# A fused attention and MLP kernel: seven products in the eighth step of the second layer too, and a flag that is read before the last output is evicted

## The chip, the core and the metric

The kernel runs on one core of one Trainium2 chip. A core has five engines that run side by side and meet at semaphores: TensorE (PE, with its weight loads shown as PEld), VectorE (DVE), ScalarE (ACT), GpSimd (POOL) and SyncE (SP), which here issues nearly all DMAs. TensorE reads SBUF and adds up in PSUM, which has eight banks; SBUF is the working memory, 128 partitions wide.

The metric is the device time of the whole kernel in microseconds. A profiled execution gives the trace; the times are of runs without the profiler.

## The reference

Attention with global and local keys and a distance bias, for 4 batches, 8 heads, 768 positions and 64 dimensions; then a two-layer MLP (3072 tokens, 512 to 2048 to 512) with h * tanh(softplus(h)):

```python
scores = scale * np.matmul(q, k.transpose(0, 1, 3, 2)) + bias     # bias: -slope * distance
scores = np.where(keep, scores, -1000000000.0)                    # keep: 8 global keys, 96 local ones
a = np.exp(scores - np.max(scores, axis=-1, keepdims=True))
x = np.matmul(a / (np.sum(a, axis=-1, keepdims=True) + 1e-09), v) # then (tokens, 512)
h = x @ w_in
g = h * np.tanh(np.where(h > 20.0, h, np.log1p(np.exp(np.minimum(h, 20.0)))))
return (g @ w_out).astype(np.float32)
```

## The kernel before

**Precision.** A float32 operand is split into a high and a low float16 part, and a product is three matmuls: high x high, high x low, low x high.

**Tiling.** The tokens run in 12 chunks (`ci`, 0 to 11) of 256, two blocks of 128 each. A chunk is attention first: scores, maximum, exponent, the split of the weights into halves (`hl`), their transposition by a DMA (`AT`), the product with v, the division (`x`), and the split and transposition of x (`xhl`, `xT`). Then the MLP runs in eight steps (`fp`, 0 to 7) of 256 hidden columns; step number m = 8 ci + fp. A step is a first-layer product on TensorE (`ph`, 24 matmuls of 256 columns), four ScalarE passes and one VectorE pass for the activation (`gf`), the split into halves (`gt`), and the second-layer product, which adds into the chunk's PSUM banks over its eight steps.

**Seven products.** A second-layer step is a 2 x 2 block product: two blocks of 128 tokens, two blocks of 128 hidden columns, and two halves (`HN` = 256) of the 512 outputs. Written out it is 8 block products, done as 12 matmuls of 512 columns (L726). From chunk 3 on, steps 0 to 6 form it from 7 block products instead, 21 matmuls of 256 columns (L717), after a scheme that needs sums of blocks: `sums_g` (L617 to L619) makes them from the activations for every step, and `whole_w`, `sums_w`, `high_s`, `low_s` once from the weights of that step. `FAST` says from which chunk each step does so; for step 7 it is `NC`, so never. The products go to four banks: 0 and 1 hold the two token blocks' own parts, 2 and 3 parts that both share. Steps 0 to 6 fill banks 2 and 3; step 7 writes banks 0 and 1 alone. So `corner` can take banks 2 and 3 to SBUF (`corners`, four pieces of 256 columns; L739 to L741) while step 7 still runs, and `evacuate` adds them to banks 0 and 1 on the way out (L753).

**The flag.** This path is valid for certain arguments and values only. Sums of everything that could have gone wrong are tested (`checks`), a scalar `done_i` is made from the tests, and behind the schedule all engines load it (L73) and branch (L74): to the end, or to a slow general kernel, `dense`. Steps k0, k1 and k3 make and test the indicators of all but the last chunk's output; k2 stands last, behind the last eviction: a matmul over the sums that the last evictions made (L807), two VectorE operations (L809, L810).

**Order.** `PROGRAM` is the order, written out by hand as some 2,100 tokens: a letter for an action, a number for chunk, block or step, and an apostrophe for the other of two engines that can do it. Each engine takes its instructions in the order in which the tokens issue them. The letters that matter here: i first-layer product, j, u, n, r, H activation, J sums of blocks, z and Z high and low halves, o second-layer product, I corner, Q eviction, Y store, g, p, X attention weights' split and transposition, T, U, V the same for x, P, G, e, m the sums and halves of the weights, w, q, v loads, O a product that only keeps TensorE busy, k checks.

Of the kernel before, what the change touches and what calls it, by code (L numbers as in the profile page):

```python
# [42 lines left out]
def tile_kernel(ctx, tc, qd, kd, qT, kT, v, n, w_in, w_out, out):  # L43
# [29 lines left out]
    left = nc.values_load(done_i[0:1, 0:1], min_val=0, max_val=1)  # L73
# [35 lines left out]
def windowed(st, tc, loc):  # L109
# [36 lines left out]
    nc.vector.memset(busy, 0.0)
# [389 lines left out]
    def high_x(n, other=False):  # L536
# [165 lines left out]
    PRODUCTS = ((0, 0, 2, 0), (2, 2, 0, 0), (6, 3, 0, 1), (1, 5, 1, 0), (3, 1, 3, 1), (5, 6, 2, 1), (4, 4, 3, 0))  # L702

    def moe_out(m):
# [8 lines left out]
        if fast(m):  # L713
            for i, k, bank, side in PRODUCTS:
                w = factor(fp, k)
                for n, (x, y) in enumerate(((0, 0), (0, 1), (1, 0))):
                    nc.tensor.matmul(pos[ci][bank][:, side * HN:(side + 1) * HN], gt[:, x, i, :], w[y], start=not begun[ci][bank], stop=n == 2 and fp == NFP - 2 and (i, k) in ((5, 6), (4, 4)))  # L717
                    begun[ci][bank] = True
            return
        for bank in range(2):  # L720
            for j in range(2):
                fb = 2 * fp + j
                for n, (x, y) in enumerate(((0, 0), (0, 1), (1, 0))):
                    cols = (slice(0, HN), slice(HN, DM)) if bank == 1 and begun[ci][1] and j == n == 0 and len(pos[ci]) > 2 else (slice(0, DM),)
                    for c in cols:
                        nc.tensor.matmul(pos[ci][bank][:, c], gt[:, x, 2 * j + 1 - bank, :], wv4[:, 2 * fb + 1, y, c], start=not begun[ci][bank], stop=last and j == 1 and n == 2)  # L726
# [6 lines left out]
    def corner(ci, other=False):  # L733
# [6 lines left out]
        nc.vector.scalar_tensor_tensor(c[:, 1:3, :], end, BACK, c[:, 3:4, :].broadcast_to([P, 2, HN]), op0=ALU.mult, op1=ALU.add)  # L740
        nc.vector.scalar_tensor_tensor(c[:, 3, :], end[:, 1, :], BACK, c[:, 1, :], op0=ALU.mult, op1=ALU.add)  # L741

    def evacuate(ci):
        po = pos.pop(ci)
        obs[ci] = raws.tile([P, DM, 2], I32, name="wr", bufs=3).bitcast(F32).rearrange("p f w -> p (f w)").rearrange("p (t m) -> p t m", t=2)
        for bank in range(2):
# [4 lines left out]
            else:  # L751
                c = corners[ci]
                nc.vector.scalar_tensor_tensor(obs[ci][:, t].rearrange("p (b m) -> p b m", b=2), po[bank].rearrange("p (b m) -> p b m", b=2), BACK, c[:, bank:bank + 3:2, :], op0=ALU.mult, op1=ALU.add, accum_out=osum[:, n:n + 1])  # L753
# [285 lines left out]
```

## Time and profile before

| what | value |
|---|---|
| median of 3 runs | 595.21 us (594.56 to 596.01) |
| the profiled execution, in all | 594.36 us |
| its span, first to last instruction | 592.5 us |
| DMA moved in the span | 73.76 MB, mean 124 GB/s |
| granted TensorE clock, mean | 1.0 |
| largest group, first-layer matmuls (L583) | 265.6 us |

The table goes from whole to part. The span is what the trace covers; the profiled execution's own time has 1.9 us more around it. TensorE's clock stands at full speed in all of the profile's slices.

### The profile page before, as it was taken

To read this page: it belongs to the slowest core of one execution; us is meant where nothing else is said; L and a number is where in the kernel's file an instruction comes from. 1 tells how busy PE (TensorE), PEld (TensorE's weight loads), DVE (VectorE), ACT (ScalarE), POOL (GpSimd) and SP (SyncE) were. 2 spreads that over 40 slices of the span, in tenths; PEclk is the share of its full clock that TensorE was granted. 3 is DMA by queue.
4 is the path that set the end of the run, shared out by engine and by line. 5 is a ranking of instruction groups with operands and counts; after the bars stand their busy time and mean duration, and the time that the engine had idled before them with its cause. 6 is when DMAs were issued, how large, how long until landed. Compare 5 with 4: busy or idle time off the path is not lost.

```text
span 592.5 us, 14936 instructions
## 1 busy us (share of the span) xinstructions
PE 577.9 (98%) x5652; PEld 466.6 (79%) x5652; DVE 489.3 (83%) x1272; ACT 478.3 (81%) x1112; POOL 261.3 (44%) x259
## 2 busy tenths in 40 slices
PE   6999999999999999999999999999999999999996
PEld 4887866567667789788889788888888888888884
DVE  6999999998999999989888986687888876663665
ACT  6999999999898998896786697677888678765661
POOL 0145422236316876552443474555563433444251
PEclk9999999999999999999999999999999999999999
DMA  9999999562562448654753653554574414240001
GB/s 228 312 276 191 254 308 242 151 148 66 118 150 55 114 95 137 100 117 122 166 115 68 126 127 80 94 118 107 88 178 58 101 38 90 54 91 19 36 2 38
DMA packets 132972, 73.76 MB, mean 124 GB/s; under 512 B 102144, under 2 KB 122624, under 8 KB 132896
## 3 DMA queue, kind: packets, MB, share of 16 engines
q1 hardware_dynamic: 132608, 72.63, 54.6%
q8 instruction: 45, 0.74, 0.5%
q14 instruction: 31, 0.25, 0.1%
q10 hardware_dynamic: 288, 0.14, 0.1%
HBM read 38.62 MB, written 6.29 MB: 76 GB/s over the span
## 4 chain that ended last, share of the span: by engine, by line
PE 77%; DVE 7%; DMA 6%; ACT 4%; issue 2%; POOL 2%; SPq 1%; DVEq 0%; POOLq 0%; ACTq 0%
PE ph L583 35%; PE pav L717 13%; PE po L717 10%; PE po L726 6%; PE sc L434 4%; PE sc L522 3%; PE pav L726 3%; DMA AT<-hl 2%; DMA vc<-v 2%; DMA wts<-w_in 1%; PE pav L518 1%; DMA qr<-qT 1%; DVE gf L607 1%; DVE gt L157 1%; DVE hl L157 1%
## 5 line engine op out<-in xcount | busy, mean ns | idle before, releaser
L583 PE MATMUL ph<-xT,wts 128*128 128x256 f16 x2304 | 265.6, 273 | 2.7 <-DVE gf L607 2.5
L583 PEld LDWEIGHTS <-wts 128*128 128x128 f16 x2304 | 222.3, 98 | 35.4 <-issue 5.4
L717 PEld LDWEIGHTS <-gt 128*128 128x128 f16 x1323 | 127.7, 98 | 16.7 <-issue 2.0
L157 POOL TENSOR_TENSOR gt<-gf,gt 128x896 f16<-128x896 f32 (+1 forms) x40 | 72.0, 1803 | 71.5 <-DVE gt L151 48.3
L590 ACT ACTIVATE e<-ph 128x512 f32<-128x512 f32 x96 | 56.4, 588 | 58.3 <-PE ph L583 55.9
L457 ACT ACTIVATE A<-A,nm 128x232 f32<-128x232 f32 (+1 forms) x192 | 88.3, 462 | 17.5 <-DVE nm L448 17.3
L607 DVE SCALAR_TENSOR_TENSOR gf<-e,ph 128x512 f32<-128x512 f32 x96 | 65.5, 682 | 32.1 <-ACT e L602 19.1
L157 POOL TENSOR_TENSOR hl<-A,hl 128x512 f16<-128x512 f32 (+1 forms) x39 | 47.5, 1224 | 78.5 <-DVE hl L151 48.4
L448 DVE CUSTOM_DVE_ANT_0 A<-sc,mb 128x232 f32<-128x232 f32 (+1 forms) x192 | 63.4, 375 | 11.7 <-PE sc L434 6.7
L726 PEld LDWEIGHTS <-gt 128*128 128x128 f16 x405 | 38.5, 98 | 40.8 <-issue 0.4
L598 ACT ACTIVATE e<-e,part 128x512 f32<-128x512 f32 x96 | 68.8, 717 | 2.1
L594 ACT ACTIVATE e<-e,ones 128x512 f32<-128x512 f32 x96 | 68.8, 717 | 1.8
L726 PE MATMUL po<-wts,gt 128*128 128x512 f16 (+1 forms) x309 | 68.4, 373 | 0.0
L157 DVE TENSOR_TENSOR gt<-gf,gt 128x896 f16<-128x896 f32 (+1 forms) x56 | 60.3, 1079 | 8.2 <-ACT gt L153 7.6
L157 POOL TENSOR_TENSOR wts<-ws,wts 128x512 f16<-128x512 f32 x22 | 30.0, 1366 | 74.0 <-ACT wts L153 28.0
L717 PE MATMUL pav<-wts,gt 128*128 128x256 f16 x378 | 62.0, 273 | 0.0
L602 ACT ACTIVATE e<-e 128x512 f32<-128x512 f32 x96 | 59.9, 624 | 1.7
L717 PE MATMUL po<-wts,gt 128*128 128x256 f16 x378 | 51.6, 273 | 0.0
L617 POOL TENSOR_TENSOR gf<-gf 128x128 f32<-128x128 f32 x41 | 23.2, 566 | 54.1 <-DVE gf L607 52.3
L151 DVE TENSOR_SCALAR gt<-gf 128x896 f16<-128x896 f32 (+1 forms) x51 | 31.5, 619 | 15.3 <-POOL gf L619 8.8
L153 ACT ACTIVATE gt<-gf 128x896 f16<-128x896 f32 (+1 forms) x45 | 36.5, 812 | 7.2 <-POOL gf L619 3.4
L457 ACT ACTIVATION_READ_ACCUMULATOR A<-A,nm 128x1 f32 x192 | 36.2, 189 | 0.0
(173 smaller groups left out, 900.8 us busy)
## 6 DMA issues: line engine op xcount, KB each, us to landing
qr<-qT SPq DMA_DIRECT2D x24, 256.0 KB
wts<-w_in SPq DMA_DIRECT2D x12, 512.0 KB
wts<-w_out SPq DMA_DIRECT2D x12, 512.0 KB
kr<-kd SPq DMA_DIRECT2D x32, 184.0 KB
out<-wr SPq DMA_DIRECT2D x11, 512.0 KB
vr<-v SPq DMA_DIRECT2D x10, 512.0 KB
vc<-vo SPq DMA_DIRECT2D x15, 192.0 KB
wr<-w_in SPq DMA_DIRECT2D x4, 512.0 KB
```

The source lines that it names most:

```text
L153: nc.scalar.activation(out, in_, AF.Copy, scale=scale)
L157: (nc.vector if other else nc.gpsimd).tensor_tensor(out, in_, high, op=ALU.subtract)
L448: nc.vector.tensor_tensor_reduce(out=A[:, j, 0:w], in0=sc[j][:, 0:w], in1=m, scale=-1.0 / (UNIT if ci < CF32 else UNIT * SQ), scalar=3.0e3 ...
L457: nc.scalar.activation(A[:, j], A[:, j], AF.Exp, bias=nm[:, h:h + 1], scale=-1.0, accum_out=rs[:, h:h + 1])
L583: nc.tensor.matmul(ph[:, j, :].rearrange("p (b t) -> p b t", b=2), wv4[:, 2 * fb, x, c * P:(c + 1) * P], xT[:, :, y * NCC + c, :], start=( ...
L590: nc.scalar.activation(mish[m]["e"], mish[m]["h"], AF.Exp, scale=1.0 / (SV * SW), accum_out=esum[:, m:m + 1])
L594: nc.scalar.activation(e, e, AF.Square, bias=ones)
L598: nc.scalar.activation(e, e, AF.Ln, bias=part, scale=SV * SW / SG / 2.0)
L602: nc.scalar.activation(e, e, AF.Exp, scale=-1.0)
L607: nc.vector.scalar_tensor_tensor(gf, mish[m]["e"], SG / (SV * SW), mish[m]["h"], op0=ALU.subtract, op1=ALU.mult, accum_out=gsum[:, m:m + 1])
L717: nc.tensor.matmul(pos[ci][bank][:, side * HN:(side + 1) * HN], gt[:, x, i, :], w[y], start=not begun[ci][bank], stop=n == 2 and fp == NFP ...
L726: nc.tensor.matmul(pos[ci][bank][:, c], gt[:, x, 2 * j + 1 - bank, :], wv4[:, 2 * fb + 1, y, c], start=not begun[ci][bank], stop=last and ...
```

## The change

Five things change.

1. `FAST` is 3 for all eight steps: step 7 of chunks 3 to 10 makes 7 products as well. The very last step (m = 95) is left out by `fast`; its products for the second token block are cut into column halves, the first half complete before the second is begun. A chunk whose eight steps are all of seven products is a `whole_chunk` (3 to 10).
2. The products within a step stand in another order: bank 2 first, then 3, 0 and 1. In a whole chunk banks 2 and 3 close in step 7 and not in step 6.
3. In a whole chunk, `corner` writes one quarter of the output itself, with its sum into `osum3`, and `evacuate` the other three quarters. `corner` now stands behind the chunk's last product.
4. The last chunk's evictions have no sum. The flag tests instead the activations: `gsum` times 0 plus `esum`, summed (`worst`, in k1), so all is known before step 95's products. The load of the flag is token k4, ahead of Q11; its bounds test is left out.
5. Split copies of x take their buffers from the ring of three of the attention weights (`hl`) and no longer from two of their own; a buffer `four` holds step 7's weight sums. `PROGRAM` is written anew throughout.

```diff
-    left = nc.values_load(done_i[0:1, 0:1], min_val=0, max_val=1)
+        left = windowed(st, tc, locals())
...
-    FAST = (3,) * 7 + (NC,)
+    FAST = (3,) * 8
...
+    four = cp.tile([P, 2, 4, DM // 2], F16, name="four")
...
-        xhl = at.tile([P, 2, DM], F16, name="xhl")
+        xhl = at.tile([P, 2, 2, W], F16, name="hl", bufs=3).rearrange("p a b w -> p a (b w)")
...
-        return ci >= FAST[fp]
+        return ci >= FAST[fp] and m != NC * NFP - 1
+
+    def whole_chunk(ci):
+        return all(fast(ci * NFP + fp) for fp in range(NFP))
...
-    PRODUCTS = ((0, 0, 2, 0), (2, 2, 0, 0), (6, 3, 0, 1), (1, 5, 1, 0), (3, 1, 3, 1), (5, 6, 2, 1), (4, 4, 3, 0))
+    PRODUCTS = ((0, 0, 2, 0), (5, 6, 2, 1), (3, 1, 3, 1), (4, 4, 3, 0), (2, 2, 0, 0), (6, 3, 0, 1), (1, 5, 1, 0))
...
-            for i, k, bank, side in PRODUCTS:
+            ends = {2: 1, 3: 3} if fp == NFP - 2 and not whole_chunk(ci) else {2: 1, 3: 3, 0: 5, 1: 6} if last else {}
+            for q, (i, k, bank, side) in enumerate(PRODUCTS):
...
+        end = ci == NC - 1 and last
+        for bank, c in ((0, slice(0, DM)), (1, slice(0, HN)), (1, slice(HN, DM))) if end else ((0, slice(0, DM)), (1, slice(0, DM))):
...
+        if whole_chunk(ci):
+            into, total = out_tile(ci)[:, 0, HN:], osum3[:, ci:ci + 1]
+            nc.vector.scalar_tensor_tensor(into, end[:, 1, :], BACK, c[:, 1, :], op0=ALU.mult, op1=ALU.add, accum_out=total)
+            return
...
+                pieces = (slice(0, 1),) if bank and whole_chunk(ci) else (slice(0, 1), slice(1, 2)) if bank and ci == NC - 1 else (slice(0, 2),)
+                for k in pieces:
+                    total = osum[:, n:n + 1] if ci < NC - 1 else None
...
-            nc.vector.reduce_max(worst, esum, axis=AX.X)
+            nc.vector.scalar_tensor_tensor(seen, gsum, 0.0, esum, op0=ALU.mult, op1=ALU.add, accum_out=worst)
...
-            pe = ps.tile([1, 2], F32, name="sc")
-            nc.tensor.matmul(pe, ones, osum[:, 2 * NC - 2:], start=True, stop=True)
...
+            done.append(nc.values_load(L.done_i[0:1, 0:1], min_val=0, max_val=1, skip_runtime_bounds_check_because="the value is a product of comparisons"))
...
-        "F": lambda i: tc.mark_branch_hint_location("general", engines=[E.PE, E.Activation, E.DVE]),
+        "F": lambda i: tc.mark_branch_hint_location("general", engines=[E.PE, E.Activation, E.DVE, E.SP]),
...
-        J91 r93 H93 j92 u92 z91' n92 i94 J93' r92 j94 u94 Z91' H92 J92' o90 z92' Z92 n94 z93' r94 H94 i95 J94 o91 j95 Z93' o92 o93 z94' u95 n95 Z94 r95 H95 k1
-        z95 Z95' k3 o94 I11 o95 Q11 k2
+        F0 j93 u93 n93 Y10 J89' z89' Z90 Z89 H91 i92 r93 J91 j92 H93 z91' u92 i94 J93 n92 Z91 j94 r92 H92 o89 J92' z92' u94 o90 z93' n94 Z92' r94 o91 i95 j95
+        o92 H94 u95 J94' Z93' n95 z94' k0 Z94 o93 r95 H95 k1 z95' Z95 k3 o94 I11' o95 k4 Q11
```

What the order does at three places, in the instructions of one engine (line, operation, out<-in, size; behind an underscore is the buffer's number).

VectorE at the end of the program, before: the flag's first part, the corner of chunk 11, the two evictions with their sums (`osum`), the two operations on the check of these sums, the flag's load and the branch.

```order
L804 SCALAR_TENSOR_TENSOR v_125<-v_125,fl 1x1
L739 TENSOR_TENSOR vr<-vr 128x256
L740 SCALAR_TENSOR_TENSOR vr<-pav_8820,vr 128x512
L741 SCALAR_TENSOR_TENSOR vr<-pav_8820,vr 128x256
L753 SCALAR_TENSOR_TENSOR wr,osum<-po_8817,vr 128x512
L753 SCALAR_TENSOR_TENSOR wr,osum<-po_8818,vr 128x512
L809 TENSOR_SCALAR last<-sc 1x2
L810 SCALAR_TENSOR_TENSOR done_i<-last,v_125 1x1
L73 TENSOR_LOAD done_i
L74 COMPARE_AND_BRANCH
```

The same place after (the line numbers are the changed file's):

```order
L830 SCALAR_TENSOR_TENSOR done_i<-v_129,fl 1x1
L751 SCALAR_TENSOR_TENSOR vr<-pav_8919,vr 128x512
L756 SCALAR_TENSOR_TENSOR vr<-pav_8919,vr 128x256
L832 TENSOR_LOAD done_i
L776 SCALAR_TENSOR_TENSOR wr<-po_8916,vr 128x512
L776 SCALAR_TENSOR_TENSOR wr<-po_8917,vr 128x256 x2
L73 COMPARE_AND_BRANCH
```

The flag is complete ahead of the corner, its load has moved ahead of the evictions, these have no sum and the second is in two halves; the corner's first sum has gone to GpSimd.

VectorE at the end of chunk 10 (step 87 is its last), before: the activation of step 90, a low half, the corner on banks 2 and 3 (`pav`), the evictions of banks 0 and 1 (`po`), a check.

```order
L607 SCALAR_TENSOR_TENSOR gf,gsum<-e,ph 128x512
L157 TENSOR_TENSOR gt<-gf,gt 128x896
L740 SCALAR_TENSOR_TENSOR vr<-pav_8307,vr 128x512
L741 SCALAR_TENSOR_TENSOR vr<-pav_8307,vr 128x256
L753 SCALAR_TENSOR_TENSOR wr,osum<-po_8304,vr 128x512
L753 SCALAR_TENSOR_TENSOR wr,osum<-po_8305,vr 128x512
L784 TENSOR_SCALAR ind<-osum 128x22
```

After:

```order
L609 SCALAR_TENSOR_TENSOR gf,gsum<-e,ph 128x512
L750 TENSOR_TENSOR vr<-vr 128x256
L751 SCALAR_TENSOR_TENSOR vr<-pav_8368,vr 128x512
L754 SCALAR_TENSOR_TENSOR wr,osum_117<-pav_8368,vr 128x256
L776 SCALAR_TENSOR_TENSOR wr,osum<-po_8365,vr 128x512
L776 SCALAR_TENSOR_TENSOR wr,osum<-po_8366,vr 128x256
L151 TENSOR_SCALAR gt<-gf 128x896
```

The corner's first sum is here on VectorE, its last operation writes output, and the second eviction is half as wide. On TensorE one first-layer step (i93) stands between o87 and o88, the next chunk's first product.

SyncE at the start, before: the first loads of queries, keys, weights and values.

```order
L175 DMA qr<-qT 128x2x256
L178 DMA kr<-kd 64x2x264
L335 DMA wts<-w_in 128x4x256
L175 DMA qr<-qT 128x2x256
L178 DMA kr<-kd 64x2x264 x2
L215 DMA vo<-v 128x2x512
```

After:

```order
L1058 BRANCH_PREFETCH_HINT
L175 DMA qr<-qT 128x2x256
L178 DMA kr<-kd 64x2x264
L335 DMA wts<-w_in 128x4x256 x2
L175 DMA qr<-qT 128x2x256
L178 DMA kr<-kd 64x2x264 x2
L215 DMA vo<-v 128x2x512
```

A hint stands ahead of the first load, and a second weight load ahead of the second queries and keys and of the first values.

More of the change, by code (lines that the diff above doesn't have):

```diff
@@ L693, in factor @@
         a, b = 4 * fp + 1, 4 * fp + 3
+        if fp == NFP - 1 and k in (1, 4, 5, 6):
+            return [four[:, y, max(k - 3, 0), :] for y in range(2)]
         if k < 4:
@@ L713, in moe_out @@
         if fast(m):
-            for i, k, bank, side in PRODUCTS:
+            ends = {2: 1, 3: 3} if fp == NFP - 2 and not whole_chunk(ci) else {2: 1, 3: 3, 0: 5, 1: 6} if last else {}
+            for q, (i, k, bank, side) in enumerate(PRODUCTS):
                 w = factor(fp, k)
                 for n, (x, y) in enumerate(((0, 0), (0, 1), (1, 0))):
-                    nc.tensor.matmul(pos[ci][bank][:, side * HN:(side + 1) * HN], gt[:, x, i, :], w[y], start=not begun[ci][bank], stop=n == 2 and fp == NFP - 2 and (i, k) in ((5, 6), (4, 4)))
+                    nc.tensor.matmul(pos[ci][bank][:, side * HN:(side + 1) * HN], gt[:, x, i, :], w[y], start=not begun[ci][bank], stop=n == 2 and ends.get(bank) == q)
                     begun[ci][bank] = True
             return
-        for bank in range(2):
+        end = ci == NC - 1 and last
+        for bank, c in ((0, slice(0, DM)), (1, slice(0, HN)), (1, slice(HN, DM))) if end else ((0, slice(0, DM)), (1, slice(0, DM))):
             for j in range(2):
@@ L723, in moe_out @@
                 for n, (x, y) in enumerate(((0, 0), (0, 1), (1, 0))):
-                    cols = (slice(0, HN), slice(HN, DM)) if bank == 1 and begun[ci][1] and j == n == 0 and len(pos[ci]) > 2 else (slice(0, DM),)
-                    for c in cols:
-                        nc.tensor.matmul(pos[ci][bank][:, c], gt[:, x, 2 * j + 1 - bank, :], wv4[:, 2 * fb + 1, y, c], start=not begun[ci][bank], stop=last and j == 1 and n == 2)
+                    nc.tensor.matmul(pos[ci][bank][:, c], gt[:, x, 2 * j + 1 - bank, :], wv4[:, 2 * fb + 1, y, c], start=not begun[ci][bank], stop=last and j == 1 and n == 2 and c.stop == DM)
                     begun[ci][bank] = True
@@ L752, in evacuate @@
                 c = corners[ci]
[L753 removed]
+                pieces = (slice(0, 1),) if bank and whole_chunk(ci) else (slice(0, 1), slice(1, 2)) if bank and ci == NC - 1 else (slice(0, 2),)
+                for k in pieces:
+                    total = osum[:, n:n + 1] if ci < NC - 1 else None
+                    nc.vector.scalar_tensor_tensor(obs[ci][:, t].rearrange("p (b m) -> p b m", b=2)[:, k], po[bank].rearrange("p (b m) -> p b m", b=2)[:, k], BACK, c[:, bank:bank + 3:2, :][:, k], op0=ALU.mult, op1=ALU.add, accum_out=total)
             if ci == NC - 1:
@@ L777, in windowed @@
     worst = cp.tile([P, 1], F32, name="worst")
+    seen = cp.tile([P, NG], F32, name="seen")
+    done = []
     v1 = cp.tile([1, NX - 2], F32, name="v1")
     v2 = cp.tile([1, NC], F32, name="v2")
-    v3 = cp.tile([1, 4], F32, name="v3")
+    v3 = cp.tile([1, 3], F32, name="v3")
     def checks(i):
@@ L893, in windowed @@
                 acts[c[0]](int(c[1:]))
+    return done[0]
 def dense(st, tc, loc):
```

133 lines of the change are left out of this document (70 added, 63 removed).

## The prediction, made before the changed kernel ran

> **What bounds the kernel now.** First the page: how busy each engine is, and the chain that ended last.
>
> ```profile
> PE 577.9 (98%) x5652; PEld 466.6 (79%) x5652; DVE 489.3 (83%) x1272; ACT 478.3 (81%) x1112; POOL 261.3 (44%) x259
> PE 77%; DVE 7%; DMA 6%; ACT 4%; issue 2%; POOL 2%; SPq 1%; DVEq 0%; POOLq 0%; ACTq 0%
> ```
>
> TensorE (PE) is busy 577.9 of 592.5 us and holds 77% of the chain. Matmul ends are modelled, so I don't trust 98% alone; the list of what PE waited for decides.
>
> ```profile
> PE sc L434 <- DMA kr<-kd: 4.0, 1, 4.0
> PE ph L583 <- DVE gf L607: 2.5, 3, 1.2
> PE po L401 <- DVE AT L146: 1.3, 1, 1.3
> PE sc L807 <- DVE wr L753: 0.8, 1, 0.8
> PE sc L522 <- DMA AT<-hl: 0.8, 2, 0.4
> PE pav L518 <- DMA vc<-v: 0.7, 1, 0.7
> ```
>
> The columns are the total, the number and the longest wait. 4.0 + 1.3 us pass before the first keys are there, 0.8 us lie in the tail, and only 2.5 + 0.8 + 0.7 = 4.0 us are lost in the 580 us between. So PE's own work sets the time; a microsecond less of it is a microsecond less of span, if the new order feeds PE as well.
>
> **Term 1, the products.** A step of 8 x 3 products was merged into 12 matmuls of 512 columns, one of them cut in two; it becomes 7 x 3 = 21 matmuls of 256. Both kinds stand in the trace, the wide ones in the eighth step, the narrow ones in the seven others. Chain in order of time (start, us, what), then the timeline of PE:
>
> ```profile
> 554.29 0.98 PE pav L717 x9
> 555.27 2.59 PE po L726 x13
> ```
> ```profile
> 427.93 0.49 PE L717 MATMUL pav<-wts,gt 128*128 128x256 f16 x3
> ...
> 430.23 2.78 PE L583 MATMUL ph<-xT,wts 128*128 128x256 f16 x24
> ```
>
> The wide step takes 2.59 us. A whole narrow step runs from 427.93 to 430.23: 2.30 us, 109 ns a matmul (0.98 / 9 in the chain too). Each converted step saves 0.29 us. Chunks 3 to 10 convert, eight steps; the last step of chunk 11 stays wide (its second half is cut into halves, the same columns). 8 x 0.29 = **-2.3 us**. The upper bound of the gain is this, since no product goes elsewhere; the lower one is zero if PE waits where the work was.
>
> [...]
>
> **Term 2, the tail.** Before, the flag sums the last chunk's output: evict, matmul (L807), two VectorE operations, load of the flag, branch. Timeline, the lines L73 and L74 by themselves, and the stretches of the DMA:
>
> ```profile
> 584.68 2.76 PE L726 MATMUL po<-wts,gt 128*128 128x512 f16 x13
> 586.44 0.42 DVE L741 SCALAR_TENSOR_TENSOR vr<-pav,vr 128x256 f32<-128x256 f32 x1
> 587.47 0.69 DVE L753 SCALAR_TENSOR_TENSOR wr<-po,vr 128x512 f32<-128x512 f32 x1
> 587.49 1.05 SPq L758 DMA_DIRECT2D out<-wr  x2
> 588.63 0.21 DVE L810 SCALAR_TENSOR_TENSOR done_i<-last,v 1x1 int32<-1x1 f32 x1
> ```
> ```profile
> L73 DVEq TENSOR_LOAD <-done_i x1: 832/832/832, 588.9 to 588.9; - x1
> L74 SPq COMPARE_BRANCH  x1: 58/58/58, 590.0 to 590.0; - x1
> L74 SPq EVENT_SEMAPHORE  x8: 17/17/17, 590.5 to 591.1; - x8
> ```
> ```profile
> 589.00:590.00 1.00, 0.00 (x0) 0.00 (x0) 0.00 (x0) 0.00 (x0) 0.00 (x0) 1.00 0.75 277
> 590.00:591.00 1.00, 0.00 (x0) 0.00 (x0) 0.00 (x0) 0.00 (x0) 0.00 (x0) 1.00 0.03 8
> ```
>
> The last product ends at 584.68 + 2.76 = 587.44, the span at 592.5: 5.06 us. From SyncE's branch (590.0) to the end are 2.5 us. The second store is issued when the last eviction is done (587.47 + 0.69 = 588.16), its issue ends at 587.49 + 1.05 = 588.54, and its data move until almost 590.0: 1.8 us from the issue's start.
>
> After, call the end of the last product T. The last eviction has 256 columns: 0.42 us (L741's form), without a sum to read; the store is issued at T + 0.46 and its data landed at T + 2.3. The flag was loaded earlier, so SyncE branches behind the issue (0.38 us), at T + 0.85; by the branch alone the span would end at T + 0.85 + 2.5 = T + 3.35. But SyncE closes with eight semaphore waits (590.5 to 591.1), the stores' among them, and these now wait for the landing. What lay behind them before is 592.5 - 590.5 = 2.0 us from the first and 1.4 from the last, so the end is at T + 3.7 to T + 4.3; I take the middle, T + 4.1 with a little for completion. The tail gains 5.06 - 4.1 = **-0.95**; bounds -1.7 (branch alone) and -0.7.
>
> Two waits are added ahead of T. The check matmul (L794, L820 after) needs chunk 11's last activations. Timeline:
>
> ```profile
> 575.06 0.49 PE L717 MATMUL pav<-wts,gt 128*128 128x256 f16 x3
> 578.15 0.69 DVE L607 SCALAR_TENSOR_TENSOR gf<-e,ph 128x512 f32<-128x512 f32 x1
> 579.12 1.09 DVE L791 TENSOR_SCALAR ind<-gsum 128x94 f32<-128x94 f32 x1
> 582.03 0.41 PE L794 MATMUL sc<-ind,ones 128*1 128x145 f32 x2
> ```
>
> The last first-layer step ended at 575.06; the indicators were ready at 579.12 + 1.09 = 580.21, which is 5.15 us later, and three product steps (6.97 us) covered that. In the new program the step before, o91, stands ahead of i95, and two steps, 4.6 us, are left as cover. PE waits 5.15 - 4.6 = 0.55 us, or nothing if the 1.09 us (for 94 columns) does not recur; I take +0.3. Behind it the VectorE queue is: ten flag operations, the corner (its sum now on GpSimd, behind the last step's low half), the flag load of 0.83 us, three evictions. If the load holds the queue, bank 0's eviction starts 0.5 us late and the end with it; if it runs while the corner executes, it costs nothing. I take +0.2. Sum of the tail: -0.95 + 0.3 + 0.2 = **-0.45**, bounds -1.7 and +0.4.
>
> **Term 3, the start.** SyncE has one hint more ahead of its first load, no row of its own; between nothing and the nearest row, the branch's 58 ns, I take +0.06. It now sends a second 512 KB weight load ahead of the second pair of query and key loads and of the first values.
>
> ```profile
> 2.93 5.47 DMA qr<-qT
> 12.06 0.71 PE L434 MATMUL sc<-kr,qr 64*128 64x128 f32 x8
> 6.00:12.00 6.00, 6.00 (x25) 3.38 (x25) 5.62 (x34) 5.03 (x21) 0.00 (x0) 1.00 1.09 296
> ```
>
> At 296 GB/s, 524 KB are 1.8 us. The queries landed at 8.4, their first product ran at 12.06: 3.7 us of cover. The values have less, perhaps +0.6; against it, the 0.7 us wait for vc may go, as one weight load fewer stands ahead of it. I take 0 with these ends, and **+0.1** with the hint.
>
> **Term 4, added work on other engines.** Eight steps more need the three sums (two of 128 columns, one of 256: 0.29 + 0.43 + 0.29 = 1.0 us by the medians on VectorE), and their high and low halves have 896 columns and not 512.
>
> ```profile
> L619 DVE TENSOR_TENSOR gf<-gf x22: 291/293/1865, 188.4 to 575.4; 128x128 f32<-128x128 f32 x22
> L618 DVE TENSOR_TENSOR gf<-gf x22: 424/425/1299, 187.5 to 575.0; 128x256 f32<-128x256 f32 x22
> L641 DVE TENSOR_TENSOR vr<-wts x6: 1219/1225/1475, 138.7 to 193.9; 128x1024 f32<-128x1024 f16 x6
> 190.00:200.00 10.00, 9.28 (x116) 7.00 (x115) 9.72 (x14) 9.93 (x20) 7.99 (x8) 1.00 0.43 97
> 500.00:510.00 10.00, 10.00 (x103) 9.01 (x101) 4.93 (x16) 8.27 (x23) 3.80 (x4) 1.00 0.37 69
> ```
>
> Past 250 us VectorE has room, and a step has at least one 2.6 us first-layer step of cover, so I cost this at nothing there. The weights of the eighth step are prepared once: 1.2 us on VectorE for the whole (L641) and about as much for the low halves, near 185 us, where VectorE is 97% busy in the row of 190; that is the third rival. At a chunk's end the corner now starts behind the last products, not a step earlier:
>
> ```profile
> L153 ACT ACTIVATE vr<-pav x9: 574/580/597, 242.4 to 584.5; 128x512 f32<-128x512 f32 x9
> L740 DVE SCALAR_TENSOR_TENSOR vr<-pav,vr x9: 691/692/693, 245.1 to 585.7; 128x512 f32<-128x512 f32 x9
> L753 DVE SCALAR_TENSOR_TENSOR wr<-po,vr x18: 678/684/691, 248.3 to 587.5; 128x512 f32<-128x512 f32 x18
> ```
>
> The copy (0.58) hides beside the other banks' products, since bank 2 closes first. From bank 3's last product: sum 0.43, 0.69, 0.42, evictions 0.68 and 0.42, together 2.6 us, with three accumulators to read about 2.9; 9 products (0.98 us) still run then, so VectorE is done 1.9 us past the step. The tightest boundary, chunk 10's, has one 2.62 us step on PE there, and the next chunk writes bank 2 first. No wait, with 0.7 us to spare.
>
> **Sum:** -2.3 - 0.45 + 0.1 = -2.7 us (rounded). The profiled execution took 594.36 us in all (span 592.5); 594.36 - 2.7 = 591.7. The median of the runs shown is 0.85 above it, so on that scale 595.21 - 2.7 = **592.5**.
>
> **Rivals.**
> - *The new order also removes waits.* Of the 4.0 us of inner waits half go and the tail's two waits don't come: 592.5 - 2.0 - 0.5 = 590.0 to 591. For it: the order is new throughout. Against: nothing in the rows shows that it aims at these. 13 in 100.
> - *The preparation at 185 us is not hidden.* Its 2.5 us on VectorE all reach PE: 595.0. For it: PE already waits at 197 and VectorE is at 97%. An operation of VectorE there can take far longer than its median: L619's third number is 1865 ns against 293. [...] 19 in 100, time 594 to 596.4.
> - *Slower: the shared ring.* The 20 split copies of x lose their own two buffers and join the ring of three that the 80 attention copies turn in. Each must wait until a transposition three places back has left.
>
> ```profile
> ACT hl L153 <- DMA AT<-hl: 3.6, 3, 2.0
> DVE hl L151 <- DMA AT<-hl: 3.0, 2, 2.4
> ```
>
>   Such waits exist: 6.6 us in 5, 1.3 each, now off PE's path. If every chunk from 2 to 11 gets one and half of it reaches the chunk's first step on PE, that is 10 x 0.65 = +6.5: 599.0. It decides once it costs over 4.0 us, 0.4 a chunk. Against: PE waited only 0.8 us for these transpositions. 10 in 100.
> - *The saved products are none:* if weight loads (one for each matmul) set PE's pace, 21 loads replace 13, and the kernel is slower by 8 x 8 x 0.098 = 6.3 us less the tail: some 601. PE's spacing of 109 and 216 ns for 256 and 512 columns speaks against it. 2 in 100.
>
> ```profile
> L717 PEld LDWEIGHTS <-gt 128*128 128x128 f16 x1323 | 127.7, 98 | 16.7 <-issue 2.0 <-ACT A L457 0.2
> ```
>
> **Chances.** Forecast 56 in 100 (591 to 594.0), then 13, 19, 10 and 2. The smallest difference that a measurement here tells from none is about 0.2%, 1.2 us: 594.0 and 596.4. Faster: 54 + 13 + 3 = 70; within: 2 + 14 = 16; slower: 2 + 10 + 2 = 14. The range 590.0 to 596.0 leaves out the shared ring and the loads (12), the third rival's end (3) and some of the first's (5).
>
> **What will show it.** Right: PE's busy time lower by about 2.3 us; 21 matmuls of 256 columns at 109 ns in the eighth step from chunk 3; no matmul on osum; the flag load ahead of the last evictions; some 4.1 us from the last product to the end. Wrong: a wait of PE at the check matmul over 0.6 us; new waits of PE near 185 to 210 us, or of the first-layer matmuls (ph) at the start of chunks; waits for AT<-hl above 0.8 us on PE; waits of po or pav products for VectorE at a chunk's start.

## The result, and the profile after

| | median | runs |
|---|---|---|
| before, measured beside it | 595.19 us | 6, 594.53 to 596.36 |
| after | 599.28 us | 6, 599.02 to 600.25 |

The ratio is 1.0069, with a 95% interval from 1.0055 to 1.0082: the changed kernel is 4.1 us slower (3.3 to 4.9). The forecast was 592.5 us, from 590 to 596: the sign is wrong.

The engines' line of the page of after, whose span is 597.2 us:

```profile
PE 577.4 (97%) x5716; PEld 474.0 (79%) x5719; DVE 503.9 (84%) x1291; ACT 482.1 (81%) x1119; POOL 273.6 (46%) x271
```

Read it as span less busy time. Before, TensorE (PE) was idle for 592.5 - 577.9 = 14.6 us; now for 597.2 - 577.4 = 19.8. So 5.2 us of new idle time stand against 0.5 us less of work. VectorE (DVE) is busy 14.6 us longer, GpSimd (POOL) 12.3. What TensorE waited for, after (total, number, longest):

```profile
PE sc L436 <- DMA kr<-kd: 4.5, 1, 4.5
PE ph L585 <- DVE gf L609: 3.9, 5, 2.1
PE po L403 <- DVE AT L146: 1.3, 1, 1.3
PE ph L564 <- DVE xT L553: 1.3, 1, 1.3
PE sc L436 <- DVE xmax L535: 1.1, 1, 1.1
PE sc L436 <- DVE nm L450: 1.1, 2, 0.8
PE pav L729 <- POOL gt L157: 0.8, 1, 0.8
```

The first line is the start, where the first keys come later (4.0 before). Of the others all but the one of `po` are new or longer than before, and behind each stands VectorE or GpSimd. The busy time by stretches says where: after each stretch its length, then TensorE, its weight loads, VectorE, ScalarE and GpSimd, the granted clock and the DMA's share; before first, then after.

```profile
30.00:60.00 30.00, 29.02 (x246) 23.60 (x246) 28.83 (x89) 29.07 (x80) 15.15 (x12) 1.00 1.01 232
60.00:250.00 190.00, 187.89 (x1756) 137.23 (x1754) 180.08 (x418) 178.30 (x404) 91.77 (x80) 1.00 0.65 149
300.00:350.00 50.00, 49.98 (x534) 42.47 (x532) 42.69 (x108) 37.56 (x86) 22.79 (x24) 1.00 0.50 104
450.00:500.00 50.00, 50.00 (x538) 42.85 (x537) 37.59 (x102) 37.92 (x85) 20.61 (x23) 1.00 0.34 66
```
```profile
30.00:60.00 30.00, 27.83 (x222) 22.52 (x223) 27.80 (x83) 26.83 (x73) 12.87 (x11) 0.94 0.89 221
60.00:250.00 190.00, 187.97 (x1763) 138.49 (x1762) 178.79 (x417) 181.07 (x407) 95.95 (x84) 1.00 0.65 151
300.00:350.00 50.00, 46.70 (x514) 40.22 (x512) 44.10 (x102) 38.49 (x91) 23.32 (x27) 1.00 0.54 120
450.00:500.00 50.00, 48.87 (x537) 42.72 (x534) 42.16 (x107) 38.95 (x88) 23.92 (x22) 1.00 0.36 69
```

TensorE loses 1.2 us at 30 to 60, nothing from there to 250, 3.3 at 300 to 350, 1.1 at 450 to 500. The first stretch also shows a clock of 0.94, which the table of before never does. The timeline of TensorE there (start, duration, and in brackets the idle time ahead), and two of its stretches:

```profile
46.13 2.78 PE L585 MATMUL ph<-xT,wts 128*128 128x256 f16 x24
50.19 0.63 PE L564 MATMUL ph<-ident,x 128*128 128x128 f32 x4 [1.27 <-DVE xT L553]
51.66 2.12 PE L436 MATMUL sc<-kr,qr 64*128 64x232 f32 x8 [0.85 <-DVE nm L450]
```
```profile
52.00:54.00 2.00, 2.00 (x9) 1.21 (x8) 1.97 (x4) 2.00 (x8) 1.16 (x1) 0.53 0.83 262
54.00:56.00 2.00, 2.00 (x12) 1.45 (x11) 2.00 (x4) 2.00 (x5) 0.00 (x0) 0.61 0.21 78
```

Two waits, 1.27 and 0.85 us, and then the granted clock is one half for 3.4 us (52.1 to 55.6, read from slices of 0.5 us): eight score matmuls take 2.12 us and not 1.05. So the stop costs its 2.1 us of waits and, estimated as half of the 3.4 us, 1.7 more. Before, the product of step 0 (12 matmuls, 2.75 us) stood in this gap; now it stands at 57.8 us.

At 302 us, VectorE's queue after, then GpSimd's:

```profile
301.82 2.19 DVE L157 TENSOR_TENSOR gt<-gf,gt 128x896 f16<-128x896 f32 x1
303.94 2.07 DVE L157 TENSOR_TENSOR hl<-A,hl 128x512 f16<-128x512 f32 x1
305.93 0.67 DVE L609 SCALAR_TENSOR_TENSOR gf<-e,ph 128x512 f32<-128x512 f32 x1
```
```profile
301.18 1.89 POOL L157 TENSOR_TENSOR gt<-gf,gt 128x896 f16<-128x896 f32 x1 [1.10 <-DVE gt L151]
303.09 2.36 POOL L157 TENSOR_TENSOR wc<-kr,wc 128x736 f16<-128x736 f32 x1
```

Both low halves on VectorE lie beside one on GpSimd and take 2.19 and 2.07 us; their medians are 1.08 and 0.69. The activation (`gf`) stands behind them, and TensorE waits 2.07 us for it. The trace shows the overlap and the longer times; that the one causes the other is inferred.

Behind 250 us TensorE has four waits over 0.3 us, which end at 306.7, 342.8, 346.6 and 478.0 us. The corners of chunks 4, 5 and 8 run at 294, 343 and 476 us, so all four lie at a corner or within 13 us behind one.

### The profile page after: what moved, and what is told of

Same layout as the page of the kernel before. It is cut to its first block, busy times and chain, and to the rows that moved or that the text cites. A ratio compares the mean times of both kernels' runs of the same rounds, so it can differ in the third digit from the quotient of the medians.

```text
span 597.2 us, 15161 instructions
## 1 busy us (share of the span) xinstructions
PE 577.4 (97%) x5716; PEld 474.0 (79%) x5719; DVE 503.9 (84%) x1291; ACT 482.1 (81%) x1119; POOL 273.6 (46%) x271
## 4 chain that ended last, share of the span: by engine, by line
PE 40%; DVE 5%; ACT 2%; issue 1%; DMA 1%; POOL 1%; DVEq 0%; POOLq 0%; SPq 0%; ACTq 0%
PE ph L585 19%; PE pav L729 10%; PE po L729 7%; PE sc L436 2%; PE sc L524 1%; DMA AT<-hl 1%; DVE gt L157 1%; DVE gf L609 1%; DVE hl L556 1%; DVE gf L623 1%; ACT A L459 0%; DVE hl L157 0%; PE po L737 0%; DVE gt L151 0%; POOL gf L623 0%
## 5 line engine op out<-in xcount | busy, mean ns | idle before, releaser
L729 PEld LDWEIGHTS <-gt 128*128 128x128 f16 x1491 | 143.2, 98 | 21.5 <-issue 2.6
L157 POOL TENSOR_TENSOR gt<-gf,gt 128x896 f16<-128x896 f32 (+1 forms) x42 | 75.8, 1807 | 64.0 <-DVE gt L151 39.5
L459 ACT ACTIVATE A<-A,nm 128x232 f32<-128x232 f32 (+1 forms) x192 | 88.3, 462 | 10.7 <-DVE nm L450 10.7
L729 PE MATMUL pav<-wts,gt 128*128 128x256 f16 x402 | 66.3, 273 | 1.3 <-POOL gt L157 0.8
L157 POOL TENSOR_TENSOR hl<-A,hl 128x512 f16<-128x512 f32 (+1 forms) x31 | 36.6, 1183 | 54.5 <-DVE hl L151 30.5
L157 POOL TENSOR_TENSOR wts<-ws,wts 128x512 f16<-128x512 f32 x21 | 27.2, 1299 | 68.9 <-ACT wts L153 21.5
L622 POOL TENSOR_TENSOR gf<-gf 128x128 f32<-128x128 f32 x43 | 27.6, 641 | 67.9 <-DVE gf L609 66.8
L729 PE MATMUL po<-wts,gt 128*128 128x256 f16 x426 | 58.1, 273 | 0.0
L737 PEld LDWEIGHTS <-gt 128*128 128x128 f16 x306 | 29.3, 98 | 31.2 <-issue 0.6
L151 DVE TENSOR_SCALAR gt<-gf 128x896 f16<-128x896 f32 (+1 forms) x50 | 34.3, 688 | 16.4 <-POOL gf L624 13.1
L157 DVE TENSOR_TENSOR hl<-A,hl 128x512 f16<-128x512 f32 (+1 forms) x49 | 43.8, 898 | 4.5 <-ACT hl L153 4.2
L737 PE MATMUL po<-wts,gt 128*128 128x512 f16 (+1 forms) x210 | 46.7, 373 | 0.0
```

Source lines behind the costliest of these rows:

```text
L157: (nc.vector if other else nc.gpsimd).tensor_tensor(out, in_, high, op=ALU.subtract)
L459: nc.scalar.activation(A[:, j], A[:, j], AF.Exp, bias=nm[:, h:h + 1], scale=-1.0, accum_out=rs[:, h:h + 1])
```

## The experiments

Two theories at the start. A: the loss is in the rewritten order. B: it is in the work that the seven products add on VectorE, GpSimd and ScalarE. Third, C: the shared ring. All 18 in one table; each ratio is to the runs of before on the same chip, and the last column is the ratio less one times 595.2.

| run | what | median | ratio (95%) | us |
|---|---|---|---|---|
| after | | 599.28 | 1.0069 (1.0055 to 1.0082) | +4.1 |
| e1 | after, no seven products in the eighth steps, none of their added work | 597.24 | 1.0032 (1.0017 to 1.0047) | +1.9 |
| e13 | e1, no shared ring | 597.63 | 1.0039 (1.0025 to 1.0053) | +2.3 |
| e7 | after, added work, ordinary products | 599.12 | 1.0065 (1.0052 to 1.0078) | +3.9 |
| e3 | old order, new tail, with the hint | 595.70 | 1.0003 (0.9989 to 1.0017) | +0.2 |
| e14 | e3 + added work | 601.80 | 1.0113 (1.0094 to 1.0131) | +6.7 |
| e15 | e3 + late corners | 604.10 | 1.0152 (1.0136 to 1.0167) | +9.0 |
| e9 | e5 + ring | 617.07 | 1.0374 (1.0353 to 1.0396) | +22.3 |
| e2 | whole change in the old order | 641.59 | 1.0772 (1.0743 to 1.0801) | +46 |
| e16 | after, step 0 in the gap | 597.85 | 1.0055 (1.0038 to 1.0072) | +3.3 |
| e8 | after, six entries moved | 599.11 | 1.0065 (1.0052 to 1.0078) | +3.9 |
| e18 | e16 + e8 | 598.13 | 1.0051 (1.0039 to 1.0063) | +3.0 |
| e6 | after, front of before | 600.49 | 1.0075 (1.0057 to 1.0092) | +4.5 |
| e4 | after, third weight load put back | 606.41 | 1.0179 (1.0152 to 1.0206) | +10.7 |
| e17 | before + hint for SP | 595.64 | 1.0012 (1.0004 to 1.0021) | +0.7 |
| e5 | e3 without the hint | 594.76 | 0.9989 (0.9976 to 1.0002) | -0.7 |
| e12 | after without the hint | 600.64 | 1.0098 (1.0072 to 1.0124) | +5.8 |
| e10 | e16 without the hint | 600.84 | 1.0112 (1.0089 to 1.0136) | +6.7 |
| e11 | e1, front of e10, no hint | 597.90 | 1.0055 (1.0035 to 1.0075) | +3.3 |

### The new order or the added work (e1, e7)

e1 (the entries that go out stand here in one line):
```diff
-    FAST = (3,) * 8
+    FAST = (3,) * 7 + (NC,)
...
-  P7' G7' e7 m7' J31' J39' J47' J55' J63 J71' J79' J87
```


> The changed kernel in its new order, but the eighth step multiplies in the ordinary way (twelve products 512 wide) and the sums, the wide halves and the four prepared weight blocks that only the seven products need are left out. The output is the same. Theory A (the loss is in the rewritten order): TensorE gets 8 x 0.29 = 2.3 us more work and every wait stays, 599.3 + 2.3 = 601.6 us, and at least 600.5. Theory B (the loss is in the work that the seven products add on VectorE, GpSimd and ScalarE): the waits behind 250 us go with it, and about 596.5 us is left (595.2 plus 1.3 for the late start). In the profile, A still has the waits of TensorE near 302 and 476 us, B has not.

e7, with the entries kept, the halves of the eighth steps still seven blocks wide:
```diff
-        return slice(1, 8) if fast(m) else slice(0, 4)
+        return slice(1, 8) if fast(m) else slice(0, 7) if padded(m) else slice(0, 4)
```


> The changed kernel in its new order, and with the added work of VectorE, GpSimd and ScalarE (sums, halves seven blocks wide, four prepared blocks, whose results aren't used), but the eighth step multiplies in the ordinary way. Theory B1 (the added work makes the waits behind 200 us): the waits at 302, 343, 346 and 476 us stay and TensorE gets 2.3 us more, 599.3 + 2.3 = 601.6 us. Theory B2 (the shorter products uncover work that was there anyway): the waits go as in e1, 597.2 to 598 us.

e1 lies near B: it is 2.0 us faster than after, although TensorE has about 2 us more to do (2.3 by the forecast's sum). Of the four waits behind 250 us its trace has only the first, 1.32 us and not 2.07. So B holds for most of them, but 1.9 us stay that B doesn't explain. e7 falls between its two expectations. It differs from e1 by the added work alone, and from after by the products and the form of the corners and evictions that goes with them: the added work costs 599.12 - 597.24 = 1.9 us in this order (2.0 by the ratios), and the shorter products bring nothing (599.28 against 599.12). What they save is waited for.

### What the seven products force, one part at a time in the old order (e3, e14, e15, e9, e2, e13)

e3, the tail alone:
```diff
-  k3 o94 I11 o95 Q11 k2
+  k3 o94 I11 o95 k4 Q11
```


> Of the change only its tail: the order of before with the flag's last test ahead of the last eviction, the two half evictions, and the branch hint for SP, and the order of the seven products within a step as in the changed kernel, which other steps use too. No seven products in the eighth step, the ring as before. All theories: 595.2 - 0.2 = 595.0 us, from 594.5 to 595.4. If the wait of the branch ahead of the eviction had a price, it would come out above 595.5.

Level with before, but 0.3 us above the range that was expected; e17 and e5, below, put that on the hint. e3 is the base of e14 and e15; that of e9 is e5, which is e3 without the hint. e14:
```diff
-  H31
+  H31 J31'
```
and so for 39, 47, up to 87, with the wide halves of e7.

> The order of before with the tail of the change (e3), buffers of their own, ordinary products, the corners where they were; added are only the sums of the eighth steps on GpSimd and the halves seven blocks wide. Theory B1 (this work costs time wherever it stands): 597.7 to 600 us against 595.7 of e3, with waits of TensorE for the product of g and h or for a low half near the ends of the chunks. If VectorE and GpSimd have room for it in this order: 595.7 us, within 0.5.

e15 (chunk 5; so for 3 to 9):
```diff
-  H48 I5 i50
+  H48 i50
...
-  H50
+  H50 I5
```


> e3 with one thing more: the corners of chunks 3 to 9 behind the eighth step, where the seven products force them, in place of right behind the seventh. The corner's own chain is about 2.5 us (0.57 + 0.73 + 0.69 + 0.42) beside a first-layer product of 2.6 us of the next chunk. If that covers it: 595.7 us, within 0.5. If the corners now stand in front of what the next steps need on VectorE: 597 to 599 us, with waits behind each end of a chunk.

e9: the ring of the change, and for its sake other places in the order. The expectations speak of 18 entries that stand later; against e5 it is 20, 17 of them transpositions that stand 2 to 20 places earlier, and only g69, p69 and X69 later.
```diff
-        xhl = at.tile([P, 2, DM], F16, name="xhl")
+        xhl = at.tile([P, 2, 2, W], F16, name="hl", bufs=3).rearrange("p a b w -> p a (b w)")
```


> e5 (the order of before, the tail of the change, no hint for SP, no seven products in the eighth step), but with the shared ring of three buffers for the halves of the attention and of its output, and the 18 places of the order that this ring forces, as in e2. Rival C (the ring is the price): most of e2's loss shows here too, over 610 us. Otherwise, if e2's loss comes from where the sums, the wide halves and the late corners stand in an order that was not made for them: as e5, 594.8 to 596 us.

e2: all three, with the products and the hint.

> The changed kernel's code on the order of before: only the entries that the change needs are put into it (the sums of the eighth steps, the preparation of the four blocks, the corners moved behind the eighth step, and the 18 places where the shared ring of three buffers leaves no room for an entry, which stands some places later). Theory A (order): the forecast of the change itself, 595.2 - 2.3 - 0.2 = 592.7 us, from 592 to 594. Theory B (added work): the waits come back in any order, 597 to 599 us. Rival C (the shared ring): 594.5 to 597 us, with TensorE waiting for VectorE or ScalarE where the entries were moved.

By the ratios the sums and wide halves cost 6.5 us (e14 less e3), the late corners 8.8 (e15 less e3), the ring with its moved entries 23 (e9 less e5), and all together, with what the products save, 46. e14 and e15 lie above what was expected of them, and e2 above all its expectations by over 40 us. e14's engines against e3's; its traced execution is its slowest, 604.4 us:

```profile
PE 577.8 (97%) x5655; PEld 467.0 (79%) x5655; DVE 488.6 (82%) x1271; ACT 478.0 (81%) x1112; POOL 259.9 (44%) x260
```
```profile
PE 581.1 (96%) x5655; PEld 467.9 (78%) x5655; DVE 501.8 (83%) x1271; ACT 480.2 (80%) x1112; POOL 281.7 (47%) x284
```

The 24 added operations are on GpSimd; VectorE has the same 1271, a few of them wider, and is busy 13.2 us longer; 3.2 us of that are in the groups with the wider halves. Operations that the edit doesn't touch take longer too, the low halves of the keys 1099 ns in the mean and not 939 (groups of e3, then e14):

```profile
L157 DVE TENSOR_TENSOR wc<-kr,wc 128x736 f16<-128x736 f32 (+1 forms) x13 | 12.2, 939 | 0.0
```
```profile
L157 DVE TENSOR_TENSOR wc<-kr,wc 128x736 f16<-128x736 f32 (+1 forms) x13 | 14.3, 1099 | 0.0
```

e15 adds no work at all. Yet its 1271 instructions on VectorE take 497.2 us, 8.6 more than e3's, so the added operations on GpSimd aren't the only thing that lengthens VectorE's; what it was in e15 stays open. Its longest wait for an activation, timeline of VectorE, then ScalarE, then TensorE:

```profile
422.23 1.09 DVE L157 TENSOR_TENSOR gt<-gf,gt 128x896 f16<-128x896 f32 x1
426.81 0.43 DVE L752 TENSOR_TENSOR vr<-vr 128x256 f32<-128x256 f32 x1 [3.48 <-ACT vr L153]
...
429.24 0.68 DVE L609 SCALAR_TENSOR_TENSOR gf<-e,ph 128x512 f32<-128x512 f32 x1
```
```profile
424.35 0.61 ACT L604 ACTIVATE e<-e 128x512 f32<-128x512 f32 x1
...
426.20 0.58 ACT L153 ACTIVATE vr<-pav 128x512 f32<-128x512 f32 x1
```
```profile
426.85 0.34 PE L524 MATMUL sc<-vo,AT 128*128 128x64 f16 x6
429.98 1.25 PE L585 MATMUL ph<-xT,wts 128*128 128x256 f16 x10 [2.79 <-DVE gf L609]
```

In this trace VectorE runs these in the program's order. It stands 3.48 us at the corner, for a copy that ScalarE makes at 426.20; the activation behind it had its input (`e`) at 424.96 and runs at 429.24; TensorE, which needs that one's buffer, waits 2.79. TensorE's wait list of e9 shows the same kind of wait, only longer:

```profile
PE ph L585 <- DVE gf L609: 15.4, 9, 4.5
```

Behind the longest of these waits stands the ring. ScalarE and VectorE wait until a transposition has left a buffer of it. The waits of e5, then of e9:

```profile
ACT hl L153 <- DMA AT<-hl: 4.1, 3, 2.4
```
```profile
ACT hl L153 <- DMA AT<-hl: 18.2, 11, 4.2
DVE hl L151 <- DMA xT<-hl: 6.1, 3, 3.2
```

With the smaller lines it is 7.1 us in 5 waits in e5 and 33.1 us in 20 in e9. TensorE's longest wait stands behind one of them (VectorE, then TensorE):

```profile
228.42 0.43 DVE L151 TENSOR_SCALAR hl<-A 128x512 f16<-128x512 f32 x1 [3.22 <-DMA xT<-hl]
...
234.15 0.68 DVE L609 SCALAR_TENSOR_TENSOR gf<-e,ph 128x512 f32<-128x512 f32 x1
```
```profile
234.89 4.46 PE L585 MATMUL ph<-xT,wts 128*128 128x256 f16 x24 [4.50 <-DVE gf L609]
```

VectorE stands 3.22 us at a split copy until a transposition of x has left the ring; a weight sum of 2.37 us follows, and the activation comes behind both. How the 23 us divide between the ring's waits and the moved entries wasn't separated.

e13:
```diff
-        xhl = at.tile([P, 2, 2, W], F16, name="hl", bufs=3).rearrange("p a b w -> p a (b w)")
+        xhl = at.tile([P, 2, DM], F16, name="xhl")
```


> e1 (new order, ordinary products in the eighth step, none of their added work), but the halves of the attention's output in buffers of their own, as before, in place of the shared ring. If the ring still makes something wait in the new order: 596 us or less against 597.2 of e1. If the new order is what it costs to live with the ring, and has paid for it already: 597.2 us, within 0.5.

With buffers of its own, the new order is no faster (597.63 against 597.24). So in it the ring itself holds nothing up any more: the waits of ScalarE and VectorE for its transpositions are 6.5 us in 6 in after, and were 6.6 in 5 before. The new order brings 46 us down to 4; what is left of the whole is 1.9 us in e1 and the added work.

### The stop at 50 us (e16, e10, e6)

e16, and e10 with the hint taken out (Z0, o0 and O4, a product that only keeps TensorE busy, come from later places):
```diff
-  T2' z0' g19' R3 S8 B7' t21 x2 w12 p19 O8 X17
+  T2' z0' Z0 g19' R3 S8 B7' t21 x2 w12 p19 O8 O4 o0 X17
```


> The changed kernel with its hint and with the front of e10 (step 0 multiplied in the gap at 50 us), nothing else. If the two waits and the halved clock behind them are a price of these places: 599.3 - 2.1 - 1.8 + 0.6 (what came back in e10 near 61 us) = 596.0 us, granted clock 1.00 there. If it comes back later: 598.5 to 599.5 us.

> The changed kernel without the hint for SP, and with three entries of its front moved: GpSimd makes the low half of step 0 one place sooner, and TensorE multiplies step 0 right behind the first layer of step 1, where it waited 1.27 and 0.85 us and the clock was halved for 3.5 us. If the stop at 50 us is a matter of these places: 599.3 - 1.0 (hint) - 2.1 (waits) - 1.8 (clock) = 594.4 us, granted clock 1.00 up to 290 us. If VectorE is what is late in the front whatever stands first: the waits come back before 70 us, 597 to 598.5 us.

TensorE in e16, timeline:

```profile
48.99 2.75 PE L737 MATMUL po<-wts,gt 128*128 128x512 f16 x12
51.58 0.60 PE L564 MATMUL ph<-ident,x 128*128 128x128 f32 x4
52.11 1.05 PE L436 MATMUL sc<-kr,qr 64*128 64x232 f32 x8
53.69 2.79 PE L585 MATMUL ph<-xT,wts 128*128 128x256 f16 x24 [0.53 <-DVE xT L553]
...
58.58 2.78 PE L585 MATMUL ph<-xT,wts 128*128 128x256 f16 x24 [1.74 <-DVE gf L609]
```

e16 lies between its two expectations. The gap is closed and the scores run at full speed again. But 0.53 and 1.74 us of wait follow. The mean granted clock was 0.995 to 0.997 in the six runs of after, and 0.999 or more in five of the six of e16; its median is 1.4 us lower, 0.8 by the ratios, whose intervals overlap. So the clock keeps up again, for a gain that the intervals don't set apart from none, and the waits' share mostly comes back. e8, below, leaves this place alone, and its five executions show the price better. The traced one has the two waits too, 1.26 and 0.85 us, but a clock of 1.00 behind them, and takes 597.69 us; the four others, with a mean clock of 0.995 or 0.996, take 598.99 to 599.41. e10 has the same mended front in its trace; its six times scatter from 598.4 to 603.4, and its median misses both expectations.

e6: entries 1 to 343 of the order taken from before.

> The changed kernel with the first 343 entries of its order (to about 60 us) replaced by those of the order of before; all the rest as changed. Theory A1 (the new front costs two waits of TensorE of 1.27 and 0.85 us near 50 us and, behind them, some 2 us in which the granted clock is about one half): these go, the late start of 1.2 us stays, and 599.3 - 2.4 = 596.9 us is left, with the granted clock at 1.00 from 50 to 58 us. Rival: what is gained there is waited for again at the next wait, 598.5 to 599.5 us.

A miss: the half clock comes at 58 to 62 us instead, and once more at 307 to 311.

### Places in queues, or VectorE's load (e8, e18)

```diff
-  t61 Z43' c17 i45 p60' o41 H44 j45
+  t61 Z43' c17 i45 H44 p60' o41 j45
...
-  U15 z48' y70 s64 Z49 j51 H50
+  z48' y70 s64 Z49 j51 H50 U15
...
-  J50' I5 Z48
+  Z48 J50' I5
...
-  H74 J74 W87 o70 X86 r76 W86 d23 z72' V20 o71 R21
+  H74 W87 o70 X86 r76 W86 R21 J74 d23 z72' V20 o71
```


> The changed kernel with six entries moved by a few places: at 302 us the product of g and h of step 44 goes ahead of a low half of the attention on VectorE that took 2.07 us beside GpSimd; at 340 us a subtraction goes behind the product of step 50, and GpSimd makes the low half of step 48 ahead of the sums of step 50; at 476 us the sums of step 74 go behind the rows of chunk 10. If each of these four waits of TensorE (2.07, 0.41, 0.82, 1.13 us) is a place in a queue behind a stalled operation, they go: 599.3 - 4.4 = 594.9 us. If VectorE as a whole is what is late there, they come back a few us later: 597 to 599 us.

> e16 (the changed kernel with the front mended) with the six moved entries of e8 as well. If places in queues are what the new order lost, both mends add up: 597.9 less the 1.2 us by which e8's trace was shorter, 596.6 us or less. If VectorE's work behind 290 us is what is late: 597.9 us again.

Neither gain comes; e8's median lies 0.1 us above its second expectation, e18's 0.2. e8 has the longest wait for the activation down from 2.1 to 1.5 us, but the same kind of wait comes 7 times and not 5:

```profile
PE ph L585 <- DVE gf L609: 5.0, 7, 1.5
```

e18 is level with e16. Moved places move the waits. That fits the second expectation of both, that behind 290 us VectorE's load around the ends of the chunks is what is late; with six entries moved it isn't shown.

### The start (e4, e17, e5, e12, e11)

e4: w2 (and the operation that reads it) behind q2, where before has it.
```diff
-  O13 w0 w2 O9
+  O13 w0 O9
...
-  y1 B2' q2 s2
+  y1 q2 w2 B2' s2
```


> The changed kernel with the third weight load put back behind the second q and k load (where it stood before), and the operation that reads it put behind it. If this load is what makes the first scores 1.3 us late: 599.3 - 1.3 = 598.0 us, with the first scores at about 6.0 us in the profile. If it is the hint for SP or the order of the first operations: 599.3, first scores still at 7.2 us.

Slower by 7 us, which no theory had. TensorE's wait list, the wait of VectorE behind it, and a stretch of e4:

```profile
PE sc L436 <- DVE nm L450: 7.0, 2, 6.2
```
```profile
16.96 0.43 DVE L151 TENSOR_SCALAR wc<-wts 128x512 f32<-128x512 f32 x1 [5.96 <-DMA wts<-w_in]
```
```profile
20.00:24.00 4.00, 4.00 (x19) 3.60 (x20) 2.61 (x12) 2.73 (x11) 0.00 (x0) 0.52 1.08 297
```

In the new order VectorE needs this load early: TensorE waits 6.2 us, to 18.4, and its clock is half (0.50) from 17.05 to 23.9. In this order the early load is no loss; the first scores stay at 7.2 us with it put back.

e17 and e5 are one edit in two directions; e12 is after with it.
```diff
-engines=[E.PE, E.Activation, E.DVE])
+engines=[E.PE, E.Activation, E.DVE, E.SP])
```


> The kernel before with nothing changed but the hint for SP, added. In the traces, kernels with the hint start their first scores near 7.2 us, those without near 6.0, yet at 40 us TensorE is no later with it. If the start is made good in the stage that the loads bound: 595.0 us, first scores at 7.2 us. If it reaches the end: 596.2 us.

> The tail alone as in the run before (e3), with the branch hint for SP taken out again. In e3, as in every kernel with the hint, the first scores started at 7.2 us; in the kernel before at 5.98, although both issue the same loads in the same order. If the hint makes the start late: first scores at about 6.0 us and 595.7 - 1.2 = 594.5 us. If it is something else of the tail's edit (the place of the flag's load), or the execution that was profiled: first scores at 7.2 us, 595.7 us.

> The changed kernel with nothing changed but the hint for SP, taken out. If the hint costs what e3 and e5 showed (0.94 us, first scores at 7.2 against 6.0 us): 598.3 us, first scores at 6.0 us. If the later start was made good elsewhere in the changed kernel: 599.3 us.

> e1 (new order, ordinary products in the eighth step, without their added work), without the hint and with the front of e10. If hint, front and added work are the three losses and add up: 597.2 - 1.0 - 3.9 = 592.3 us, below before (595.1). If the front's waits come back: 595.5 to 596.5 us.

The first scores, e17 and then e12:

```profile
7.11 1.23 PE L434 MATMUL sc<-kr,qr 64*128 64x128 f32 x8 [5.16 <-DMA kr<-kd]
```
```profile
5.87 1.23 PE L436 MATMUL sc<-kr,qr 64*128 64x128 f32 x8 [3.06 <-DMA kr<-kd]
```

The first scores start at 7.1 to 7.3 us in the 14 traces with the hint, and at 5.9 to 6.3 in the six without. The hint costs 0.7 us (0.2 to 1.2) in before, so some of the late start is made good. In after its removal doesn't help: e12 misses both its expectations, isn't faster than after, and scatters from 598.7 to 603.4, where after lies within 1.3. e11 has all three supposed losses out, the added work (as e1 has), the hint and the stop, and was to take 592.3 us if they add up. It isn't faster than e1. So the losses don't simply add up; why kernels in the new order scatter without the hint stays open.

## Why the prediction was wrong, step by step

**Term 1, the products (-2.3): right in TensorE's work, wrong as a gain.** Narrow matmuls went from 1323 to 1491, 168 = 8 x 21. In e16, whose clock keeps up, TensorE is busy 576.1 us, 1.8 less than before. The condition, "if the new order feeds PE as well", didn't hold, and the bound below, "zero if PE waits where the work was", is what happened: e7, without the saving, takes as long as after.

**Term 2, the tail (-0.45): right in sum, by luck.** e3 has the hint and the tail, e17 the hint alone: their ratios differ by 0.0009, -0.5 us, though the intervals overlap. From the last product to the end it takes 4.7 us in e3, 5.1 in e17, where 4.1 was forecast. The gain of 0.95 was too large, and the two added waits of 0.5 didn't come: two errors that cancel.

**Term 3, the start (+0.1): the hint was mis-sized**, +0.06 forecast, +0.7 measured in before. That the early weight load costs nothing fits: TensorE is busy 23.91 us in the first 30, and was 23.90 before.

**Term 4 is the step that failed**: "Past 250 us VectorE has room, and a step has at least one 2.6 us first-layer step of cover, so I cost this at nothing there." Measured, the added work costs 2.0 us in the new order (e7 less e1) and 6.5 in the old (e14 less e3), and in the new one the 2.3 us that the products save are waited for as well. A mean share of VectorE was taken for room, and read from one stretch: 500 to 510 us, where it is busy 4.9 us in 10. At 300 to 350, where most of the loss came, it was busy 42.7 of 50 before the change. There, after, two low halves take two and three times their median beside GpSimd (2.19 and 2.07 us), and the activation that frees TensorE's buffer stands behind them in VectorE's queue. The same for the corner: "No wait, with 0.7 us to spare" counted its own chain and not what stands behind it; alone it costs 8.8 us (e15 less e3).

**The order.** The prediction took it as neutral, apart from a rival in which it also removes waits. The parts need a new one (46 us in the old), and this one brought its own stop at 50 us, with a halved clock that no step of the prediction considered. e1 has the stop in its trace; of its twelve executions the two with a mean clock of 0.999 or more take 595.98 and 596.31 us, against a median of 597.24, so about 1 us goes with the half clock.

**The rivals.** The shared ring was given 599.0, and that is the time, by luck: its mechanism is real in the old order (e9), but the new one doesn't have it. Its waits for the ring are as long as before (6.5 us against 6.6), and in e13 buffers of its own bring nothing. The preparation at 185 us was hidden: TensorE is busy 187.97 of the 190 us from 60 to 250, before 187.89.

The sum as measured, by the ratios: e1 +1.9 us, the added work +2.0 (e7 less e1), the products +0.2 (after less e7), which is none. These are steps from one run to the next, so that they make up 4.1 is no test. Against the forecast the products miss by 2.5 us, the added work by 2.0, and e1, for which tail and start gave -0.35, by about 2.3. If the hint and the tail cost in the new order what they cost in the old (+0.7 and -0.5), which e12 and e11 don't bear out, 1.7 us are left for the order's front and the late corners; these weren't separated.

## What to carry to other kernels

Work given to an engine that is 83% busy, as VectorE was, isn't free because its mean leaves room (here it cost 2.0 us, e7 less e1): ask which instruction that frees the bounding engine stands behind it in its queue, and look at its durations beside a second engine's operations (2.19 and 2.07 us here, against medians of 1.08 and 0.69). Price what an edit forces (buffers, a later corner, a new order) one by one; in the old order each cost more than the products were to save. And a gap in TensorE of 2 us can cost nearly 4: in after 2.1 us of waits were followed by a half clock for 3.4 us, an estimated 1.7 us more.

## What was not expected of the hardware

Behind gaps in TensorE's work the granted clock fell to 0.50 for about 3.4 us, in after from 52.1 to 55.6 us, which adds an estimated 1.7 us, half of that time, to the gap. In after 2.1 us of waits (1.27 and 0.85) with 0.6 us of work between them stood ahead of it; e2 has five such dips, e4 one of 6.8 us that begins within a wait of 6.2. The same gap doesn't always bring one: the two waits at 50 us were followed by it in after and not in e8's trace, and the wait of 2.1 to 2.2 us near 305 us in the traces of e6, e7 and e12, and not in those of after, e10 and e16. What decides it, no run here tests.
